# Feature blocks 2 to 4 of the first 512 tokens: two DMA transposes in place of twelve TensorE turns, and five weight columns written by GpSimd

## The chip, the cores and the metric

The kernel runs on one core of one Trainium2 chip. The metric is the time of one execution on the device, in microseconds (us), as a median over executions; lower is better. The profile's span, from the first to the last recorded work, is about 1.8 us shorter than this time (214.1 us in the run that took 215.9).

The profile lists five engines: TensorE (PE in the profile, 1413 matmuls before, with its weight loads as PEld), VectorE (DVE, 387 instructions), ScalarE (ACT, 185), GpSimd (POOL, 13) and SyncE (SP), which here only issues DMAs. Its timeline prints what an engine waited for, where the profile shows it. A line such as SPq is a DMA issue.

## The reference

2048 tokens of 640 features go through two branches, mixed token by token by a sigmoid gate.

```python
x = A_x                                             # [1, 2048, 640] bf16
g = sigmoid((x * gate_w).sum(-1, keepdims=True))
# branch A: state-space model with a diagonal complex state of 640
dt = exp(log_dt); Lam = Lambda_re + 1j * Lambda_im
Lam_bar = exp(dt * Lam)
Bu = einsum("bld,pd->blp", x, ((Lam_bar - 1) / Lam)[:, None] * (B_re + 1j * B_im))
h[t] = Lam_bar * h[t - 1] + Bu[:, t, :]
a = 2 * einsum("blp,dp->bld", h, C_re + 1j * C_im).real + x * Dskip
# branch B: a feed-forward layer of width 1728
b = gelu(x @ w1 + b1) @ w2 + b2
return g * a + (1 - g) * b
```

## The kernel before

The tokens are cut into four chunks of 512. The program's matmuls take the token features on the partitions, so every chunk needs its x transposed: `xT[c]` is 128 x 5 x 512, five feature blocks `kd` of 128. For chunks 1 to 3 a DMA transpose makes it. For chunk 0 nothing can start before it, so x is loaded plainly and TensorE transposes it by matmuls with an identity, called turns. Each turn leaves a 128 x 128 block in PSUM, and ScalarE or VectorE copies it to SBUF.

Feed-forward weights are loaded in three column groups, `w1a` (the first 768 columns), `w1b` and `w1c`, in the order of use. The gate weights become the last column of `w1c`, so that the gate's sum falls out of the last feed-forward matmul. Loads and parameter rows, in the order of issue:

```python
load_x0(nc.sync, 0, 1, 0, KA * P)              # tokens 0-127, features 0-255; KA = 2
load_w1a(nc.scalar, 0)
load_x0(nc.sync, 1, 2, 0, KA * P)
load_w1a(nc.scalar, 1)
load_x0(nc.sync, 2, 3, 0, KA * P)
load_x0(nc.scalar, 0, H, KA * P, D)            # features 256-639 of tokens 0-255
load_x0(nc.sync, 3, 4, 0, KA * P)
load_w1a(nc.sync, 2)
# ... clear prmA, prmB; warm up ScalarE's table
rows(nc.sync, prmA[0:KS, :], A_log_dt)
rows(nc.sync, prmA[KS:2 * KS, :], A_Lambda_im)
rows(nc.sync, prmA[2 * KS:3 * KS, :], A_Lambda_re)
load_x0(nc.sync, H, TPC, KA * P, D)            # features 256-639 of tokens 256-511
nc.sync.dma_start(out=w1a34[:], in_=...)       # w1a for blocks 3 and 4
rows(nc.sync, prmB[KS:NB, :], B_b1[0:(KF - 1) * P])
rows(nc.sync, prmB[0:KS, :], gate_w)
for kd in range(KD):
    nc.sync.dma_start(out=w1b[kd][:], in_=B_w1[kd * P:(kd + 1) * P, cut1:cut2])
# ... then w1c, B^T, ...
```

`prmA` holds log_dt and Lambda as rows; one small matmul with the identity (called the prmA matmul below) turns them into columns. In every trace PE passes this matmul before it goes on with the feed-forward layer, so when its rows are late, PE waits. The start of chunk 0 on PE, where `part(kd, a)` is feature block kd for 128 tokens and six column blocks of `w1a`:

```python
def turn(p, col, a, kd):
    nc.tensor.matmul(p[:, col:col + P], lhsT=xn[0][:, a, kd * P:(kd + 1) * P], rhs=ident[:], ...)
# ... blocks 0 and 1 of tokens 0-383
turn_rest(0, pA, (nc.scalar, KA, KD))          # three turns, one copy
nc.tensor.matmul(pP[:, 0:3 * KS], lhsT=prmA[:], rhs=ident[:, 0:3 * KS], ...)
part(0, 3)
turn_rest(1, bank(), (nc.vector, KA, KD))
part(1, 3)
part(2, 0); part(2, 1)
turn_rest(2, pA, (nc.scalar, KA, KD))
turn_rest(3, bank(), (nc.vector, KA, KD))
strip(KD - 1, 0, HT, False)                    # block 4, tokens 0-255
part(2, 2); part(2, 3)
# ... then block 4 of tokens 256-511 and block 3, Gelu, w1b, w1c, and at about 21 us x B^T
```

VectorE's instruction order is fixed when the kernel is built, by a small clock model: `ck.pe` adds an estimated time for each matmul, and an output combination (`ot`, one of two buffers) is put into VectorE's queue where the model says that its matmuls are done.

## Time and profile before

| | |
|---|---|
| time, median of 3 | 215.71 us (215.52 to 215.97) |
| profiled run, span | 215.9 us, 214.1 us |
| PE busy | 98% |
| first turn / prmA matmul / first w1b matmul | 3.28 / 7.40 / 12.80 us |
| first B^T matmul | 21.08 us |

Lines from the page of the kernel before: busy time of the engines, the granted TensorE clock in 40 slices, and the engines' shares of the chain that ended last.

```profile
PE 210.6 (98%) x1413; PEld 127.4 (59%) x1413; DVE 189.1 (88%) x387; ACT 102.7 (48%) x185; POOL 1.0 (0%) x13
PEclk9999999999999999999999999999999999999999
PE 98%; DVE 0%; issue 0%
```

The timeline of PE before, from 3.2 us on: start, duration, engine, line, operation, tiles and count; an idle time before the instruction would stand in brackets.

```profile
3.28 0.42 PE L233 MATMUL bank<-ident,xn 128*128 128x128 bf16 x2
...
4.46 1.16 PE L267 MATMUL bank<-xT,w1a 128*128 128x128 bf16 x9
5.42 0.42 PE L233 MATMUL bank<-ident,xn 128*128 128x128 bf16 x2
5.63 0.98 PE L267 MATMUL bank<-xT,w1a 128*128 128x128 bf16 x12
...
7.23 0.33 PE L233 MATMUL bank<-ident,xn 128*128 128x128 bf16 x3
7.40 0.17 PE L371 MATMUL bank<-ident,prmA 128*128 128x15 bf16 x1
...
12.80 4.48 PE L267 MATMUL bank<-xT,w1b 128*128 128x512 bf16 x20
...
21.08 0.81 PE L549 MATMUL bank<-xT,BT_re 128*128 128x512 bf16 x3
```

There is no bracket (the profile prints one from 0.15 us on): PE waits for nothing from the first turn on. The nine matmuls from 4.46 to 5.42 take (5.42 − 4.46) / 9 = 107 ns each; matmuls of the same shape take 57 ns from about 6 us on. The 512-column warm-up matmuls start 427 ns apart from 1.15 us on, those of the w1b stage 216. I read this as PE's clock doubling in between, at about 5.9 us, although the granted-clock row shows full speed throughout. The packed trace agrees: its first clock record, at full speed, starts at 5.92 us, and the row draws the time ahead of any record as full.

### The profile page before, as it was taken

The page shows a single profiled execution, that of the slowest core. Times are in us where ns is not written, and L with a number is a line of the kernel's source. Part 1 is how long each engine was busy: PE and PEld are TensorE (multiplying, and loading weights), DVE is VectorE, ACT ScalarE, POOL GpSimd, SP SyncE. Part 2 cuts the span into 40 slices and gives each one's busy share as a digit, 9 for nine tenths or more (in the row PEclk, how much of TensorE's full clock was granted, in tenths as well). Part 3 has the DMA queues.
Part 4 walks back from the last instruction along what each step waited for, and adds up shares of the span by engine and source line. Part 5 has one row for each costly group of instructions (what it writes and reads, how often), then busy time and mean ns, then how long its engine had stood idle before and what let it go on. Part 6 is the DMA issues. An engine that isn't in the chain of part 4 may idle for free.

```text
span 214.1 us, 3607 instructions
## 1 busy us (share of the span) xinstructions
PE 210.6 (98%) x1413; PEld 127.4 (59%) x1413; DVE 189.1 (88%) x387; ACT 102.7 (48%) x185; POOL 1.0 (0%) x13
## 2 busy tenths in 40 slices
PE   8999999999999999999999999999999999999994
PEld 5955444454475644775457777444457687676773
DVE  1589999999998999999999999999999999993153
ACT  3499856675759579203573210455683422305100
POOL 1000000000000000000000000000000000000000
PEclk9999999999999999999999999999999999999999
DMA  6869999999000000042000005100000000100011
GB/s 191 232 147 202 207 183 287 324 211 186 0 0 0 3 0 0 17 136 109 0 3 0 0 0 183 65 0 2 3 0 14 3 0 31 61 34 0 0 66 61
DMA packets 31571, 15.84 MB, mean 74 GB/s; under 512 B 22978, under 2 KB 31554, under 8 KB 31554
## 3 DMA queue, kind: packets, MB, share of 16 engines
q1 hardware_dynamic: 30850, 14.99, 29.2%
q10 hardware_dynamic: 704, 0.62, 0.9%
q8 instruction: 11, 0.18, 0.3%
q14 instruction: 6, 0.05, 0.1%
HBM read 7.48 MB, written 2.62 MB: 47 GB/s over the span
## 4 chain that ended last, share of the span: by engine, by line
PE 98%; DVE 0%; issue 0%
PE bank L267 27%; PE bank L608 27%; PE bank L667 20%; PE bank L549 20%; PE bank L230 1%; PE bank L624 1%; PE bank L293 1%; PE bank L233 1%; DVE ot L672 0%; PE bank L358 0%; PE bank L283 0%; PE bank L396 0%; PE bank L371 0%
## 5 line engine op out<-in xcount | busy, mean ns | idle before, releaser
L608 PE MATMUL bank<-w_sb,gel 128*128 128x384 bf16 (+1 forms) x416 | 57.9, 299 | 0.0
L608 PEld LDWEIGHTS <-gel 128*128 128x128 bf16 x416 | 40.3, 98 | 17.0 <-issue 0.8
L552 ACT ACTIVATE bu<-bank 128x512 bf16<-128x512 f32 x40 | 23.6, 597 | 37.3 <-PE bank L549 37.3
L272 ACT ACTIVATE gel<-bank,colB 128x512 bf16<-128x512 f32 x52 | 33.7, 693 | 10.4 <-PE bank L267 10.1
L667 PEld LDWEIGHTS <-hs 128*128 128x128 bf16 x330 | 31.7, 98 | 11.6
L503 DVE TENSOR_TENSOR_SCAN g<-r_c,carry,v 128x512 bf16<-128x512 f32 x30 | 37.2, 1268 | 0.0
L616 ACT ACTIVATE gb<-bank,gcol 128x384 f32<-128x384 f32 (+1 forms) x32 | 15.1, 526 | 32.9 <-PE bank L608 16.4
L267 PE MATMUL bank<-xT,w1a 128*128 128x512 bf16 (+2 forms) x180 | 28.6, 315 | 0.0
L667 PE MATMUL bank<-CT_re,hs 128*128 128x320 bf16 (+2 forms) x165 | 27.1, 295 | 0.0
L667 PE MATMUL bank<-CT_im,hs 128*128 128x320 bf16 (+2 forms) x165 | 27.1, 295 | 0.0
L672 DVE SCALAR_TENSOR_TENSOR ot<-bank,gcol,gb 128x320 bf16<-128x320 f32 (+2 forms) x33 | 17.4, 531 | 9.6 <-PE bank L667 8.2
L549 PE MATMUL bank<-xT,BT_re 128*128 128x512 bf16 x100 | 24.8, 379 | 0.0
L549 PE MATMUL bank<-xT,BT_im 128*128 128x512 bf16 x100 | 24.8, 379 | 0.0
L267 PEld LDWEIGHTS <-w1a 128*128 128x128 bf16 x180 | 15.5, 102 | 11.3
L267 PE MATMUL bank<-xT,w1b 128*128 128x512 bf16 x80 | 17.9, 379 | 0.0
L549 PEld LDWEIGHTS <-BT_im 128*128 128x128 bf16 x100 | 9.8, 98 | 11.8
L582 DVE TENSOR_TENSOR bank<-xn,Dbc 128x320 f32<-128x320 bf16 (+2 forms) x33 | 14.5, 480 | 2.1 <-ACT gb L616 2.1
L549 PEld LDWEIGHTS <-BT_re 128*128 128x128 bf16 x100 | 9.6, 98 | 11.0
L484 DVE TENSOR_TENSOR v<-wa,wb 128x512 bf16<-128x512 bf16 x40 | 15.2, 421 | 0.6
L597 ACT ACTIVATE bank<-b2bc 128x384 f32<-128x384 bf16 (+1 forms) x24 | 11.7, 529 | 7.6 <-DVE ot L672 7.6
L484 DVE TENSOR_TENSOR wa<-TCOS,g 128x1024 bf16<-128x1024 bf16 x20 | 13.7, 684 | 0.1
L267 PE MATMUL bank<-xT,w1c 128*128 128x512 bf16 x60 | 13.7, 379 | 0.0
(99 smaller groups left out, 166.1 us busy)
## 6 DMA issues: line engine op xcount, KB each, us to landing
out_dram<-ot SPq DMA_DIRECT2D x15, 160.0 KB, 1.8
w_sb<-in_B_w_dram SPq DMA_DIRECT2D x1, 2080.0 KB
xn<-in_A_x_dram SPq DMA_DIRECT2D x3, 640.0 KB
w1b<-in_B_w_dram SPq DMA_DIRECT2D x5, 128.0 KB, 3.6
w1c<-in_B_w_dram SPq DMA_DIRECT2D x5, 112.0 KB, 3.2
w1a<-in_B_w_dram ACTq DMA_DIRECT2D x2, 192.0 KB, 3.0
w1a<-in_B_w_dram SPq DMA_DIRECT2D x1, 384.0 KB, 3.7
xn<-in_A_x_dram SPq DMA_DIRECT2D x4, 64.0 KB, 3.6
```

The source lines that it names most:

```text
L267: nc.tensor.matmul(p[:, t0:t1], lhsT=w, rhs=xT[c][:, kd, t0:t1], start=(kd == 0) if first is None else first, stop=(kd == last), skip_grou ...
L272: nc.scalar.activation(out=gel[c][:, kf, :], in_=p[:, :], func=ACT.Gelu_apprx_tanh, bias=b1_c[:, kf:kf + 1])
L484: nc.vector.tensor_tensor(out=o, in0=a, in1=b, op=op)
L503: nc.vector.tensor_tensor_scan(s["g"][:, ri, :], r_c[:, ks:ks + 1].to_broadcast([P, CH]), s["v"][:, ri, :], init, ALU.mult, ALU.add)
L549: nc.tensor.matmul(p[:], lhsT=BT[ks >= KSA][:, kd, (ks % KSA if ks < KSA else ks - KSA) * P:][:, 0:P], rhs=xT[c][:, kd, :], start=(kd == 0 ...
L552: nc.scalar.activation(out=bu[:, ri, :], in_=p[:], func=ACT.Identity)
L582: dve_now(ck.pe, 0.45, lambda: nc.vector.tensor_tensor(out=p[:, 0:d1 - d0], in0=xn[c][:, a, d0:d1], in1=Dbc[:, d0:d1], op=ALU.mult))
L597: nc.scalar.activation(out=v, in_=src, func=ACT.Identity)
L608: nc.tensor.matmul(p[:, col:col + d1 - d0], lhsT=gel[c][:, kf, a * P:(a + 1) * P], rhs=w2_sb[:, kf, d0:d1], start=False, stop=False, skip_ ...
L616: nc.scalar.activation(out=gbs[ti][:, d0:d1], in_=p[:, col:col + d1 - d0], func=ACT.Identity, scale=gcol[:, 1, ti:ti + 1])
L667: nc.tensor.matmul(p[:, 0:d1 - d0], lhsT=hs[c][:, j, lo:lo + P], rhs=CT[:, j % KS, d0:d1], start=False, stop=(j == 2 * KS - 1), skip_group ...
L672: nc.vector.scalar_tensor_tensor(out=ot[:, d0:d1], in0=p[:, 0:d1 - d0], scalar=gcol[:, 0, ti:ti + 1], in1=gbs[ti][:, d0:d1], op0=ALU.mult, ...
```

## The change

Its intent is to take work from PE, which sets the time. Twelve turns go, their four PSUM copies with them, and blocks 2 to 4 come from two DMA transposes of 256 tokens each (196 KB). Since a block then arrives for 256 tokens or more at once, its matmuls can be wider. The first 192 KB of the plain x load are no longer ahead of the other loads; x for the later skip term is loaded much later. The three rows of `prmA` move to ACT's queue. GpSimd writes the gate columns, from the copy in SBUF, in place of five VectorE copies from PSUM.

```diff
-    load_x0(nc.scalar, 0, H, KA * P, D)
+    rows(nc.scalar, prmA[0:KS, :], A_log_dt)
     load_x0(nc.sync, 3, 4, 0, KA * P)
     load_w1a(nc.sync, 2)
     ... warm-up of ScalarE's table
-    rows(nc.sync, prmA[0:KS, :], A_log_dt)
-    rows(nc.sync, prmA[KS:2 * KS, :], A_Lambda_im)
-    rows(nc.sync, prmA[2 * KS:3 * KS, :], A_Lambda_re)
-    load_x0(nc.sync, H, TPC, KA * P, D)
-    nc.sync.dma_start(out=w1a34[:], in_=...)
+    for a in range(0, TPC, H):
+        nc.sync.dma_start_transpose(out=xT[0][:, KA:KD, a * P:(a + H) * P], in_=x2d[a * P:(a + H) * P, KA * P:D])
+    rows(nc.scalar, prmA[KS:2 * KS, :], A_Lambda_im)
+    rows(nc.scalar, prmA[2 * KS:3 * KS, :], A_Lambda_re)
+    load_w1a(nc.sync, 4)
+    load_w1a(nc.sync, 3)
     ... prmB rows and the five w1b loads as before
-    for kd in range(KD):                                    # w1c: five DMAs
+    for t, k0, k1 in ((w1c_lo, 0, 3), (w1c_hi, 3, KD)):     # w1c: two DMAs
     ... after w2:
+    load_x0(nc.sync, 0, TPC, KA * P, D)
     ... PE:
-    turn_rest(0, pA, (nc.scalar, KA, KD))
-    turn_rest(1, bank(), (nc.vector, KA, KD))
-    part(2, 0)
-    part(2, 1)
-    turn_rest(2, pA, (nc.scalar, KA, KD))
-    turn_rest(3, bank(), (nc.vector, KA, KD))
+    strip(2, 0, HT, False)
-    strip(KD - 1, 0, HT, False)
-    part(2, 2)
-    part(2, 3)
+    strip(2, HT, CH, False)
+    strip(4, 0, CH, False)
-            for j in range(KD):
-                nc.vector.tensor_copy(out=w1c[j][:, n1c - 1:n1c], in_=pA[:, j:j + 1])
     ... after the Gelus of w1a and of two w1b banks:
+    for t, k0, k1 in ((w1c_lo, 0, 3), (w1c_hi, 3, KD)):
+        nc.gpsimd.tensor_copy(out=t[:, :, n1c - 1:n1c], in_=colB[:, k0:k1].rearrange("p (k o) -> p k o", o=1))
```

One late load of x (chunk 3) is also split in two, and one early PSUM copy goes from ScalarE to VectorE.

More of the change, by code (lines that the diff above doesn't have):

```diff
@@ L83 @@
     xT = [const.tile([P, KD, CH], BF16, name=f"xT{c}") for c in range(NCH)]
-    w1a = [const.tile([P, cut1], BF16, name=f"w1a_{kd}") for kd in range(3)]
-    w1a34 = const.tile([P, 2, cut1], BF16, name="w1a34")
-    w1a += [w1a34[:, j, :] for j in range(2)]
+    w1a = [const.tile([P, cut1], BF16, name=f"w1a_{kd}") for kd in range(KD)]
     w1b = [const.tile([P, cut2 - cut1], BF16, name=f"w1b_{kd}") for kd in range(KD)]
-    w1c = [const.tile([P, n1c], BF16, name=f"w1c_{kd}") for kd in range(KD)]
+    w1c_lo = const.tile([P, 3, n1c], BF16, name="w1c_lo")
+    w1c_hi = const.tile([P, 2, n1c], BF16, name="w1c_hi")
+    w1c = [w1c_lo[:, j, :] for j in range(3)] + [w1c_hi[:, j, :] for j in range(2)]
     w2_sb = const.tile([P, KF - 1, D], BF16, name="w2_sb")
@@ L142 @@
     load_x0(nc.sync, 2, 3, 0, KA * P)
-    load_x0(nc.scalar, 0, H, KA * P, D)
+    nc.vector.memset(prmA[:], 0.0)
+    nc.vector.memset(prmB[:], 0.0)
+    rows(nc.scalar, prmA[0:KS, :], A_log_dt)
     load_x0(nc.sync, 3, 4, 0, KA * P)
     load_w1a(nc.sync, 2)
-    nc.vector.memset(prmA[:], 0.0)
-    nc.vector.memset(prmB[:], 0.0)
     warm = const.tile([P, 1], F32, name="warm")
     nc.scalar.activation(out=warm[:], in_=nc.const_aps.tensor(1.0, [P, 1], BF16), func=ACT.Exp)
-    rows(nc.sync, prmA[0:KS, :], A_log_dt)
-    rows(nc.sync, prmA[KS:2 * KS, :], A_Lambda_im)
-    rows(nc.sync, prmA[2 * KS:3 * KS, :], A_Lambda_re)
-    load_x0(nc.sync, H, TPC, KA * P, D)
-    nc.sync.dma_start(out=w1a34[:], in_=B_w1[3 * P:KD * P, 0:cut1].rearrange("(k p) f -> p k f", p=P))
+    for a in range(0, TPC, H):
[4 more added lines that the diff above has]
+    load_w1a(nc.sync, 3)
     rows(nc.sync, prmB[KS:NB, :], B_b1[0:(KF - 1) * P])
@@ L158 @@
         nc.sync.dma_start(out=w1b[kd][:], in_=B_w1[kd * P:(kd + 1) * P, cut1:cut2])
-    for kd in range(KD):
-        nc.sync.dma_start(out=w1c[kd][:, 0:F - cut2], in_=B_w1[kd * P:(kd + 1) * P, cut2:F])
+    for t, k0, k1 in ((w1c_lo, 0, 3), (w1c_hi, 3, KD)):
+        nc.sync.dma_start(out=t[:, :, 0:F - cut2], in_=B_w1[k0 * P:k1 * P, cut2:F].rearrange("(k p) f -> p k f", p=P))
     make_identity(nc, ident[:])
@@ L248, in turn_first @@
         turn(other, a * P, a, 1)
-        turned(nc.scalar, other, a * P, a, 1, 2)
+        turned(nc.scalar if a else nc.vector, other, a * P, a, 1, 2)
     turn_first(0, pA)
@@ L327, in strip @@
             ff1_mm(banks[kf], 0, kf, kd, t0, t1, first, 3)
-    def turn_rest(a, t, *parts):
-        for k in range(KA, KD):
-            turn(t, (k - KA) * P, a, k)
-        for engine, k0, k1 in parts:
-            turned(engine, t, (k0 - KA) * P, a, k0, k1)
     HB = CH // 2
@@ L397 @@
             nc.vector.tensor_copy(out=colB[:], in_=pA[:, 0:NB])
-            for j in range(KD):
-                nc.vector.tensor_copy(out=w1c[j][:, n1c - 1:n1c], in_=pA[:, j:j + 1])
-        for kd in (4, 3):
-            ff1_mm(banks[kf], 0, kf, kd, HT if kd == 4 else 0, CH, False, 3)
+        ff1_mm(banks[kf], 0, kf, 3, 0, CH, False, 3)
     for kf in range(FA):
@@ L700 @@
     fin_a(1)
-    load_xn(3)
+    load_xn(3, 0, H)
+    load_xn(3, H, TPC)
     ssm(3)
```

## The prediction

> **What bounds it now.** TensorE. The chain of waits puts 98% of the 214.1 us span on it; the list of waits shows none of it after the start; the granted clock is full. VectorE is busy 88%, yet always ahead: chunk 0's last state tile is written at 68 us and first read by the output matmuls at 86.8, the last CT fold ends 3.3 us before them. So only PE time counts, and the change alters PE's order only before 12.8 us (the first w1b matmul).
>
> **PE work removed.** From the PE timeline: twelve 128-column turns (six took 0.34 us, three 0.17) are 0.68 us. Feature block 2 goes from 24 matmuls of 128 columns (18 take 1.14 us, 63 ns each) to 12 of 256 (about 107 ns): 1.51 to 1.28 us. Block 4, 12 of 256 to 6 of 512, is even. [...] the trace has 57, 107, 216. Sum: 0.9 us, all on the chain. Also gone: four PSUM copies (ACT 0.49, DVE 0.56 us each), five DVE column copies (0.41 us) and two bank allocations. They let the sine chain and the first Gelu (13.6 us now) start 1 to 1.5 us earlier, which only keeps ACT and DVE ahead of PE.
>
> **What it adds: a new wait.** Blocks 2 and 4 of chunk 0 are then needed from the transposes at about 8.0 us (first half) and 8.7 (second), w1a4 at 9.35, w1a3 at 10.65. SP issues in order, and every DMA waits for the one eight before it (the order of instructions shows it; before, SP waited 0.4 us for w1a0 before its sixth issue). So transpose 1 issues at about 3.5 us, transpose 2 at 4.4, w1a4 at 5.4, w1a3 at 5.9. The first BT transpose (328 KB) took 5.2 us from issue to landing: 2.7 until its burst at about 290 GB/s, 1.2 in it, about 1.2 after. Estimate for 196 KB from these: 4.6 us, so landings at about 8.1 and 9.1, and w1a4, queued behind, at 9.6 to 10. [...] this trace has 290 GB/s in BT bursts against 370 to 390 in the plain w2 load, and gaps between transposes. I expect PE to wait about 0.5 us in all, mostly for transpose 2.
>
> Smaller risks: Lambda_re now leaves ACT's queue behind the warm-up and w1a1 (about 4.6 us against 4.17), needed at 7.2; w1b2 to w1b4 are issued after transpose 2 and w1a4 land, needed from 12.8 to 13.6. Smaller gain: 192 KB less in front of the first x tiles and w1a1, up to 0.3 us. Moved without effect: the rest of xn[0] (needed at 84 us), the GpSimd columns (needed at 20 us), the split late xn load.
>
> **Prediction.** 0.9 saved, 0.5 given back: 215.3 us, 8 in 10 between 214.6 and 216.2. Faster by over 2%: 0.01; within 2%: 0.97; slower by over 2%: 0.02.
>
> **What would show it.** First w1b matmul at about 12.4 us instead of 12.8, and every later PE stage earlier by the same amount, with unchanged lengths. PE waiting before the block-2 matmuls for the xT transposes (0.1 to 0.8 us in all). First Gelu near 12.2 us. If transposes land by 8.0 and 8.7, w1b starts at 11.9 and the time is near 214.8; if the second lands after 9.9, the change loses.
>
> **What would make it wrong.** Transposes much slower or faster beside plain loads than the BT ones; [...] a BT or w1b landing that turns into a second stall; PE, once earlier, catching up with DVE.

## More of the kernel before

SP's queue before, where the weights are issued:

```profile
5.25 0.40 SPq L154 DMA_DIRECT2D w1a<-in_B_w_dram  x1
...
6.71 2.26 SPq L158 DMA_DIRECT2D w1b<-in_B_w_dram  x5
```

## The result and the profile after

The kernel after took 215.89 us (median of 6 runs, 215.63 to 216.52). The kernel before took 215.86 us in the same rounds (6 runs, 215.52 to 216.16). The ratio is 1.0007 with a 95% interval of 0.9988 to 1.0025: the same time. Ratios in this document are the mean time of one kernel's runs over that of the other's runs of the same rounds, so not quite the ratio of the medians quoted.

The profiled execution after (216.52 us, the slowest of the six; span 214.7 us) has on its page:

```profile
PE 208.7 (97%) x1372; PEld 124.9 (58%) x1383; DVE 188.2 (88%) x381; ACT 102.3 (48%) x182; POOL 1.9 (1%) x15
DVE 70%; PE 22%; DMA 4%; issue 2%; ACT 1%; DVEq 0%
```

PE is less busy than before, but the chain that ended last no longer runs along PE alone: it leads through DVE and 4% of DMA. (11 of the 1383 matmuls have no record in this trace, so its busy time is a little low.) The PE timeline after:

```profile
4.25 0.67 PE L269 MATMUL bank<-xT,w1a 128*128 128x128 bf16 x9
...
5.78 0.83 PE L269 MATMUL bank<-xT,w1a 128*128 128x128 bf16 x12
7.18 0.17 PE L366 MATMUL bank<-ident,prmA 128*128 128x15 bf16 x1 [0.57 <-issue]
...
9.59 1.89 PE L269 MATMUL bank<-xT,w1a 128*128 128x512 bf16 x8 [0.24 <-DMA w1a<-in_B_w_dram]
...
11.99 1.46 PE L269 MATMUL bank<-xT,w1b 128*128 128x512 bf16 x6
13.96 3.20 PE L269 MATMUL bank<-xT,w1b 128*128 128x512 bf16 x14 [0.52 <-DMA w1b<-in_B_w_dram]
...
20.96 0.81 PE L538 MATMUL bank<-xT,BT_re 128*128 128x512 bf16 x2
```

The first w1b matmul starts 0.81 us earlier than before, but the first B^T matmul only 0.12 us earlier. Three waits stand in between or ahead: for the parameter rows, for a w1a load and for a w1b load. None is for a transpose. (The profile does not name what ended the first one, it prints "issue". That it was the rows is inferred: the matmul reads `prmA`, whose last row was issued at 4.31 us, 2.8 us before PE's weight load at 7.15, and in r9_gp below, whose rows landed by 6.3, there is no such wait.) Here the clock had doubled by 4.25 us: nine matmuls take (4.76 − 4.25) / 9 = 57 ns, where 4.76 us is the start of the next turn.

SP's queue after shows why w1b came late:

```profile
3.39 2.65 SPq L151 DMA_TRANSPOSE xT<-in_A_x_dram  x2
6.08 1.06 SPq L127 DMA_DIRECT2D w1a<-in_B_w_dram  x2
...
8.00 2.25 SPq L159 DMA_DIRECT2D w1b<-in_B_w_dram  x5
```

Two transposes hold the queue for 2.65 us, 1.3 us each, where a plain load of 192 KB holds it for 0.43. The w1b loads are issued from 8.00 us on and not from 6.71, 1.3 us later, while PE wants them earlier. The last of the five was issued at 8.54 us before and 9.82 after, and landed 4.4 us later in both traces, at 12.9 and 14.2. So in this pair the delay is one of issue and not of transfer (other traces: 3.6 and 4.0 us from issue to landing before, 4.1 to 4.6 after); experiments below test it.

Later in the program the kernel after lost a little more. VectorE after, around 98 and 135 us:

```profile
98.58 0.55 DVE L661 SCALAR_TENSOR_TENSOR ot<-bank,gcol,gb 128x320 bf16<-128x320 f32 x1 [1.42 <-DMA out_dram<-ot]
...
134.75 0.53 DVE L661 SCALAR_TENSOR_TENSOR ot<-bank,gcol,gb 128x320 bf16<-128x320 f32 x1
136.61 0.55 DVE L661 SCALAR_TENSOR_TENSOR ot<-bank,gcol,gb 128x320 bf16<-128x320 f32 x1 [1.32 <-DMA out_dram<-ot]
137.07 1.27 DVE L492 TENSOR_TENSOR_SCAN g<-r_c,carry,v 128x512 bf16<-128x512 f32 x1
...
174.55 0.90 DVE L571 TENSOR_TENSOR bank<-xn,Dbc 128x320 f32<-128x320 bf16 x2
```

The same stretch before:

```profile
134.20 0.52 DVE L672 SCALAR_TENSOR_TENSOR ot<-bank,gcol,gb 128x320 bf16<-128x320 f32 x1
134.64 1.27 DVE L503 TENSOR_TENSOR_SCAN g<-r_c,carry,v 128x512 bf16<-128x512 f32 x1
135.83 0.98 DVE L672 SCALAR_TENSOR_TENSOR ot<-bank,gcol,gb 128x320 bf16<-128x320 f32 x2
...
172.55 0.90 DVE L582 TENSOR_TENSOR bank<-xn,Dbc 128x320 f32<-128x320 bf16 x2
```

Before, a scan stands between the two output combinations; after, the combination comes first and must wait for its buffer's store. No line of the change touches this code. The build-time clock model saw other matmul widths at the start, its `ck.pe` moved by 0.036 us, and three places in VectorE's fixed order swapped. VectorE reached the seeding of the output banks at 174.55 us and not 172.55, and PE waited for it, its only wait for VectorE after the start:

```profile
175.10 0.84 PE L656 MATMUL bank<-CT_re,hs 128*128 128x320 bf16 x5 [0.52 <-DVE bank L571]
```

### The profile page after: what moved, and what is told of

Same layout as the page of the kernel before. It is cut to its first block, busy times and chain, and to the rows that moved or that the text cites. A ratio compares the mean times of both kernels' runs of the same rounds, so it can differ in the third digit from the quotient of the medians.

```text
span 214.7 us, 3526 instructions
## 1 busy us (share of the span) xinstructions
PE 208.7 (97%) x1372; PEld 124.9 (58%) x1383; DVE 188.2 (88%) x381; ACT 102.3 (48%) x182; POOL 1.9 (1%) x15
## 4 chain that ended last, share of the span: by engine, by line
DVE 70%; PE 22%; DMA 4%; issue 2%; ACT 1%; DVEq 0%
DVE g L492 19%; PE bank L656 10%; DVE wa L473 10%; DVE wb L473 10%; PE bank L597 7%; DVE v L473 6%; DVE hs L473 6%; DMA out_dram<-ot 4%; DVE bank L571 3%; PE bank L269 3%; DVE ot L661 3%; DVE CT_re L461 2%; DVE CT_im L461 2%; DVE g L421 1%; PE bank L232 1%
## 5 line engine op out<-in xcount | busy, mean ns | idle before, releaser
L656 PEld LDWEIGHTS <-hs 128*128 128x128 bf16 x330 | 31.7, 98 | 12.4 <-issue 0.7
L661 DVE SCALAR_TENSOR_TENSOR ot<-bank,gcol,gb 128x320 bf16<-128x320 f32 (+2 forms) x33 | 17.6, 535 | 12.4 <-PE bank L656 9.5
L269 PE MATMUL bank<-xT,w1a 128*128 128x512 bf16 (+2 forms) x158 | 27.0, 322 | 0.5 <-DMA w1a<-in_B_w_dram 0.2
L269 PEld LDWEIGHTS <-w1a 128*128 128x128 bf16 x162 | 13.8, 98 | 12.2 <-DMA w1a<-in_B_w_dram 0.3
L473 DVE TENSOR_TENSOR wb<-TSIN,g 128x1024 bf16<-128x1024 bf16 x20 | 13.7, 685 | 0.0
```

The source lines that it names most:

```text
L269: nc.tensor.matmul(p[:, t0:t1], lhsT=w, rhs=xT[c][:, kd, t0:t1], start=(kd == 0) if first is None else first, stop=(kd == last), skip_grou ...
L473: nc.vector.tensor_tensor(out=o, in0=a, in1=b, op=op)
L656: nc.tensor.matmul(p[:, 0:d1 - d0], lhsT=hs[c][:, j, lo:lo + P], rhs=CT[:, j % KS, d0:d1], start=False, stop=(j == 2 * KS - 1), skip_group ...
L661: nc.vector.scalar_tensor_tensor(out=ot[:, d0:d1], in0=p[:, 0:d1 - d0], scalar=gcol[:, 0, ti:ti + 1], in1=gbs[ti][:, d0:d1], op0=ALU.mult, ...
```

## The experiments

Twelve runs were made, in four calls; runs of one call are on one chip and share their runs of the kernel before, whose medians were 215.46, 215.93, 215.60 and 215.39 us. Differences of a few tenths of a microsecond in a median are not more than scatter here, so I rest the argument on stages of the traces. In each profiled run the span splits in two at the first B^T matmul: the start up to it, and the rest, which is the same work in all kernels. Where a quoted expectation gives a theory the letter E, it is the moving clock step, told below.

| run | kernel | clock doubles at about | first B^T matmul | rest of span |
|---|---|---|---|---|
| first look | before | 5.9 us | 21.08 | 193.0 |
| r5_before | before | 6.7 | 21.55 | 193.1 |
| r11_before_look | before | 3.9 to 4.2 | 20.44 | 193.1 |
| first look | after | 3.6 | 20.96 | 193.7 |
| r1_again | after | 4.2 | 20.65 | 193.3 |
| r2_dveorder | after, old VectorE order | 4.0 | 21.01 | 193.1 |
| r3_ot3 | after, three ot buffers | 6.4 | 20.73 | 193.1 |
| r4_w1btwo | after, w1b in two DMAs | 6.5 | 20.61 | 194.5 |
| r6_cols | before, columns by GpSimd | 6.2 | 21.20 | 193.2 |
| r9_gp | after, parameters by GpSimd | 5.1 | 19.87 | 194.1 |
| r10_gp_w1b | r9 and w1b in two DMAs | 6.7 | 20.64 | 193.1 |
| r12_gp_sp | r9 and w2 in four DMAs | 6.0 | 20.34 | 193.2 |

"Rest" is the span less the column to its left (214.7 − 20.96 = 193.7). The clock's step is the start of the trace's first full-clock record, and agrees within 0.1 us with the spacing of 128-column matmuls, 107 ns before it and 57 after; r11_before_look has no such record, so there it is read from the spacing alone. (Some expectations below were written with a rougher reading, 4.2 us for all three early steps.)

### The unaltered kernels once more

r1_again is the kernel after, r5_before and r11_before_look are the kernel before, without an edit.

> The changed kernel, unaltered. Theory A: its runs fall in two groups. Where VectorE loses time to late output DMAs (2.7 us in the profiled run), the first output matmuls of chunk 2 wait about 0.5 us and the run takes about 216.4; where it does not, the run takes 215.6 to 215.9. In every profile the first w1b matmul starts near 12.0 us, then PE waits about 0.5 us for w1b and reaches the BT matmuls at 20.9 to 21.0, only 0.1 us before the kernel before. Rival B: one group, scatter of the chip alone; ratio 1.000 and the profile shows the same 0.5 us wait at chunk 2 every time.

> The kernel before, unaltered, for a second profile. Theory E: the runs of one kernel differ mostly by the moment at which PE's matmuls of 128 columns go from 107 ns to 57 ns apart (5.9 us in the first profile of before; 4.2 us in three and 6.5 us in two profiles of the changed kernel). Where it comes near 4.2 us here, BT matmuls start at 20.3 to 20.5 and the run takes 215.0 to 215.3; where it comes at 5.9 us or later, they start at 21.1 or later and the run takes 215.9 or more. So before's fast runs form two groups 0.8 us apart. Rival: the groups come from DMA landings and the BT start does not go with the moment of the step.

> The kernel before once more, for one profile. Theory E: with the clock step near 4.2 us BT starts at 20.2 to 20.5 and the run takes 215.0 to 215.4; with a step at 5.9 us or later 21.0 to 21.6 and 215.9 to 216.4.

Measured: r1_again 215.99 us (215.65 to 216.62), ratio 1.0024 (0.9999 to 1.0049). r5_before 216.06 us (215.48 to 216.43), ratio 1.0003 (0.9982 to 1.0023), so no bias of the comparison shows. r11_before_look 215.23 us. The two groups expected of r1_again do not stand out in its six runs, and its first B^T matmul came at 20.65 us and not at 20.9 to 21.0; the expectations for r5_before and r11_before_look held.

The kernel before is not one time but a range, and its traces say why. Lines of r5_before (216.35 us in its profiled run):

```profile
4.63 1.17 PE L267 MATMUL bank<-xT,w1a 128*128 128x128 bf16 x9
...
21.55 0.81 PE L549 MATMUL bank<-xT,BT_re 128*128 128x512 bf16 x3
```

and of r11_before_look (215.23 us), the same stages:

```profile
4.45 0.67 PE L267 MATMUL bank<-xT,w1a 128*128 128x128 bf16 x9
...
20.44 0.81 PE L549 MATMUL bank<-xT,BT_re 128*128 128x512 bf16 x3
```

Nine matmuls take 1.17 us in one and 0.67 in the other; the clock doubled early in r11 and late in r5, and the first B^T matmul differs by 21.55 − 20.44 = 1.11 us. The times differ by 216.35 − 215.23 = 1.12, and the rest of the span is equal. The other two traces with this PE work fit in between: 5.9 us and 21.08, and r6_cols with 6.2 and 21.20. So the kernel before follows the clock's step all the way. The step moves from run to run without any edit: 3.9 to 4.2, 5.9 and 6.7 us in the three traces of the kernel before, and 3.6 to 6.7 us over all kernels. What sets its moment is not shown.

The kernel after does not follow the step in the same way. Its four early-stepping and late-stepping traces (first look, r1 and r2 at 3.6 to 4.2; r3 at 6.4, equal to the kernel after up to 90 us) have the first B^T matmul at 20.96, 20.65, 21.01 and 20.73. After a late step that is 0.8 us earlier than r5_before, whose first turn itself started 0.18 us later (3.47 us against 3.29), and 0.5 earlier than r6_cols, with the PE work of before, a start at 3.29 and a step at 6.2. After an early step it is 0.2 to 0.6 us later than r11_before_look, the only early trace of before, although the first turn there started 0.2 us later. With an early step, PE runs into the landing of loads and waits for them; with a late one PE itself is slow and waits little (r3: only 0.20 us, for w1b). Early waits were 0.57, 0.84 and 0.76 us for the parameter rows, 0.24, 0.19 and 0.24 for w1a. The landings set the pace of the start.

### How much PE work is gone: both kernels with the data already there

The chain's start is held on PE until all early loads have landed. The same edit goes into both kernels: VectorE runs 16 timed operations, PE runs 46 dummy matmuls meanwhile, and then one matmul that needs VectorE's result. In both traces the clock is up at the start of the chain: nine 128-column matmuls take 0.50 us from 17.12 us on, 56 ns each.

```diff
+    tim = const.tile([P, D], F32, name="tim")
+    go = const.tile([P, P], BF16, name="go")
+    nc.vector.memset(tim[:], 0.0)
+    for _ in range(16):
+        nc.vector.tensor_tensor(out=tim[:], in0=tim[:], in1=tim[:], op=ALU.mult)
+    nc.vector.tensor_copy(out=go[:], in_=tim[:, 0:P])
+    for _ in range(46):
+        nc.tensor.matmul(pA[:, 0:512], lhsT=ones(P), rhs=ones(512), start=True, stop=True)
+    nc.tensor.matmul(pA[:, 0:P], lhsT=go[:], rhs=ones(P), start=True, stop=True)
```

> The kernel before, held: a chain of sixteen VectorE operations (about 14 us) ahead of the first turn, with 46 more dummy matmuls, so that all loads have landed and PE's clock is up before the first turn. Theory E and F (in the first 14 us the changed kernel runs at the pace of DMA landings and of the clock step, not of PE's work): from the first turn to the first BT matmul 16.9 to 17.2 us without any PE wait, and the scatter of the fast runs falls below 0.5 us. To be compared with r8_hold_after.

> The changed kernel, held in the same way. Theory F (the PE work saved, 0.9 us, is real and is hidden by landings): from the first turn to the first BT matmul 0.8 to 1.0 us less than in r7_hold_before, and the whole run 0.7 to 1.0 us faster than r7_hold_before. Rival G (the longer matmuls and the transposes save PE nothing): both equal within 0.2 us.

The PE timeline of r7_hold_before, first turn and first B^T matmul:

```profile
16.24 0.28 PE L242 MATMUL bank<-ident,xn 128*128 128x128 bf16 x2
...
33.04 1.24 PE L558 MATMUL bank<-xT,BT_re 128*128 128x512 bf16 x5
```

and of r8_hold_after:

```profile
16.25 0.27 PE L244 MATMUL bank<-ident,xn 128*128 128x128 bf16 x2
...
32.09 1.24 PE L547 MATMUL bank<-xT,BT_re 128*128 128x512 bf16 x5
```

With no wait for a load in it, this stretch is 16.80 us before and 15.84 us after. The change removes 0.96 us of PE work. The whole times show it too: five of six runs of r7 lie at 227.81 to 227.85 us, three of r8 at 226.90 to 226.93, 0.90 us less. The other runs, one of r7 (229.32) and three of r8 (228.53 to 228.54), are 1.5 and 1.6 us longer. I have no profile of such a run, but the record lists the mean granted clock of each: 0.991 to 0.993 in these four, 0.998 to 1.000 in the other eight. A clock lower by 0.7 to 0.9% over 227 us is 1.6 to 2.0 us, the size of the gap; what lowered it stays open. So the medians of this pair prove nothing; I use the stretch and the low groups. (The expected scatter below 0.5 us failed by these runs, and the stretch before is just under the expected 16.9 to 17.2.)

### The gate columns alone

r6_cols is the kernel before with w1c in two DMAs and the columns written by GpSimd.

```diff
-            for j in range(KD):
-                nc.vector.tensor_copy(out=w1c[j][:, n1c - 1:n1c], in_=pA[:, j:j + 1])
+    for t, k0, k1 in ((w1c_lo, 0, 3), (w1c_hi, 3, KD)):
+        nc.gpsimd.tensor_copy(out=t[:, :, n1c - 1:n1c], in_=colB[:, k0:k1].rearrange("p (k o) -> p k o", o=1))
```

> The kernel before with only the other part of the change: w1c in two DMAs and the gate weight columns written by GpSimd. All theories: no PE wait for GpSimd, the five VectorE copies (0.4 us) gone, PE stages of the same length, time equal to before's within 0.2 us. If this run is slower by 0.3 us or more, the columns have a part in the missing gain.

It took 215.79 us (215.17 to 216.23), ratio 0.9995 (0.9976 to 1.0014), no PE wait. This part neither gives nor costs anything that can be seen.

### Late losses: VectorE's order and the output buffers

r2_dveorder is the kernel after with the constant that the clock model had lost:

```diff
+    ck.pe += 0.036
     for kf in range(FA):
         ff1_act(banks[kf], 0, kf)
```

r3_ot3 is the kernel after with a third output buffer, so that a combination need not wait for a store:

```diff
-            ot = fwork.tile([P, D], BF16, name="ot", bufs=2)
+            ot = fwork.tile([P, D], BF16, name="ot", bufs=3)
```

> Changed kernel, with 0.036 us added to the build-time clock so that VectorE's instruction order is that of the kernel before (three swaps undone). Theory A1 (the swap that puts the third output tile before a scan makes VectorE wait for the output DMA): VectorE's wait near 135 us vanishes, its lag at 172 us is below 1.5 us, PE does not wait before chunk 2's output matmuls, and no run is above 216.1; median 215.6. Rival A2 (late output DMAs are chance, order has no part): same spread as r1_again.

> Changed kernel with three output tiles in place of two, so that VectorE does not wait for an output DMA. Theory A: no VectorE wait on out_dram in the middle of the kernel, no PE wait at chunk 2, median 215.6 and highest below 216.1. If the slow runs stay, the DMA wait is not what makes them. It is not expected to gain more than 0.3 us over the median of the changed kernel, since PE reaches BT only 0.1 us earlier.

r2_dveorder took 215.37 us (215.06 to 216.17), ratio 0.9994 (0.9966 to 1.0022); r3_ot3 215.70 us (215.33 to 216.26), ratio 1.0010 (0.9985 to 1.0035). Neither trace has a VectorE wait for a store, neither has a PE wait at the output of chunk 2, and both have 193.1 us for the rest of the span, as before. The kernel after has 193.7 and 193.3, with a PE wait at that point of 0.52 us in the first trace; in r1_again that stage started 0.16 us late. So the late loss is real in the traces (that stage starts 0.16 to 0.68 us late, counted from the first B^T matmul), and goes with either cure. In the medians it is at the edge: r2 is the lowest of the first call, but its interval holds 1. Both expectations also set 216.1 us as a ceiling, and the highest runs were 216.17 and 216.26, so the slowest runs are not shown to come from the late loss.

### The w1b wait

r4_w1btwo is the kernel after with w1b loaded by two DMAs of three and two blocks, to shorten SP's issue:

```diff
-    for kd in range(KD):
-        nc.sync.dma_start(out=w1b[kd][:], in_=B_w1[kd * P:(kd + 1) * P, cut1:cut2])
+    for t, k0, k1 in ((w1b_lo, 0, 3), (w1b_hi, 3, KD)):
+        nc.sync.dma_start(out=t[:], in_=B_w1[k0 * P:k1 * P, cut1:cut2].rearrange("(k p) f -> p k f", p=P))
```

> Changed kernel with w1b in two DMAs (three blocks, two blocks) in place of five: same bytes, SP issues done about 1.3 us earlier. Theory C (SP's issue time, 2.65 us of it for the two transposes, delays w1b): the wait of 0.5 us for w1b vanishes or halves, BT matmuls start at 20.3 to 20.6, time 0.3 to 0.6 us below r1_again. Rival D (the DMA engines are behind with the bytes, transposes moving slower than plain loads): w1b blocks 3 and 4 land at 13.9 to 14.2 as before and the BT start stays at 20.9 or later.

SP's queue and PE's timeline in r4_w1btwo:

```profile
7.95 0.41 SPq L161 DMA_DIRECT2D w1b_lo<-in_B_w_dram  x1
8.41 0.49 SPq L161 DMA_DIRECT2D w1b_hi<-in_B_w_dram  x1
```

```profile
12.32 1.47 PE L271 MATMUL bank<-xT,w1b_lo 128*128 128x512 bf16 x6
13.63 1.03 PE L271 MATMUL bank<-xT,w1b_hi 128*128 128x512 bf16 x4
```

The issue of w1b takes 0.95 us in place of 2.25, the bytes are the same, and no w1b wait appears after the first w1b matmul. About 0.2 us is lost just ahead of it: the first w1b matmul starts 0.85 us after the last w1a group and not 0.65, and its weight load waits for the larger first DMA, which landed 4.3 us after issue. This supports SP's issue time as the cause of the w1b wait. It is not a clean proof: the clock's step was late in this run (6.5 us), so PE also came later. r9_gp below is the better test. The time to issue is not small beside the DMA here: in the kernel after, two transposes held the issuing queue for 2.65 us, with landings of 3.2 and 4.0 us after issue (2.6 to 3.2 us for the plain 192 KB w1a loads of the same trace).

The whole kernel was slower all the same, 216.91 us (216.84 to 217.02), ratio 1.0063 (1.0040 to 1.0086). The start was not the cause (20.61 us). The rest of the span was 194.5 us, 1.4 more than the usual 193.1. It has a PE wait of 0.37 us at the output of chunk 2, as in the kernel after, and a long end: 4.07 us from the start of the last group of matmuls to the end of the span, against 3.1 to 3.4 in the traces of other runs.

### Parameters on a queue of their own, and the long end

r9_gp is the kernel after with the five parameter rows issued by GpSimd and the constant of r2; r10_gp_w1b adds the two w1b loads of r4; r12_gp_sp is r9_gp with the w2 load cut in four.

```diff
-    rows(nc.scalar, prmA[0:KS, :], A_log_dt)      # and the four other rows on scalar and sync
+    rows(nc.gpsimd, prmA[0:KS, :], A_log_dt)      # all five, after the memsets of tf
+    rows(nc.gpsimd, prmA[KS:2 * KS, :], A_Lambda_im)
+    rows(nc.gpsimd, prmA[2 * KS:3 * KS, :], A_Lambda_re)
+    rows(nc.gpsimd, prmB[KS:NB, :], B_b1[0:(KF - 1) * P])
+    rows(nc.gpsimd, prmB[0:KS, :], gate_w)
+    ck.pe += 0.036
 # r12_gp_sp also:
-    for k0, k1 in ((0, KF - 1),):
+    for k0, k1 in ((0, 4), (4, 7), (7, 10), (10, KF - 1)):
```

> Changed kernel with the five small parameter rows on GpSimd's queue (off the SP and ACT queues, so the transposes no longer wait for a DMA eight places earlier), and VectorE's order as in r2_dveorder. Theory F: the wait for prmA (0.57 to 0.84 us where the clock steps up early) is gone, prmA is read before 7.0 us there, SP issues w1b from about 7.0 us instead of 8.0, the w1b wait goes, BT matmuls start at 20.1 to 20.6, the run takes 215.0 to 215.5 with all runs under 216.0: 0.2 to 0.8 us faster than before. Rival (something else holds the first 14 us): BT start stays at 20.7 to 21.0.

> r9_gp with w1b in two DMAs as well. Theory C: BT matmuls at or before r9_gp's, within 0.2 us. Open is the 0.8 us that r4_w1btwo showed after its last output DMA; if the two-DMA form of w1b makes it, this run shows it again (about 0.8 us above r9_gp with PE ending at the same time); if not, it came from elsewhere.

> The kernel of r9_gp (the changed kernel, with the five parameter rows loaded by the GpSimd queue and the build-time constant that keeps VectorE's old order) with the second big weight of the feed-forward loaded in four DMAs, so that SyncE's queue has 58 issues and not 55. Theory (an instruction fetch of the last stores' queue falls after the last output in kernels with 55 or fewer rows there, and the end waits for it): first B^T matmul between 19.9 and 20.7 us without a PE wait, the end 3.1 to 3.4 us after the last matmul (4.31 in r9_gp), span 213.0 to 213.7, median 0.2 to 0.8 us below the kernel before (ratio 0.996 to 0.999). Rival (the long end of r9_gp has another cause): the end stays at 4.0 us or more, the ratio at 1.002 to 1.006, and the cause is open.

The start of r9_gp is the best of all traces. Its w1b issue on SP's queue, and its PE timeline:

```profile
6.87 2.33 SPq L154 DMA_DIRECT2D w1b<-in_B_w_dram  x5
```

```profile
6.97 0.17 PE L366 MATMUL bank<-ident,prmA 128*128 128x15 bf16 x1
7.00 4.08 PE L269 MATMUL bank<-xT,w1a 128*128 128x128 bf16 x33
...
11.59 4.48 PE L269 MATMUL bank<-xT,w1b 128*128 128x512 bf16 x20
...
19.87 1.24 PE L539 MATMUL bank<-xT,BT_re 128*128 128x512 bf16 x5
```

PE waits for nothing, and the first B^T matmul is at 19.87 us, 1.2 us before the first trace of before (whose clock stepped 0.8 us later). The transposes still hold SP's queue (2.66 us), but without the parameter rows w1b is issued from 6.87 us, 1.13 earlier than in the kernel after; its last block lands at 11.9 and not at 14.2 (about 1.05 us of that is the earlier issue, the rest a faster transfer), and PE, which comes for it earlier than in any other trace, does not wait. Yet r9_gp took 216.05 us (215.77 to 218.29), ratio 1.0052 (1.0017 to 1.0088), where 215.0 to 215.5 was expected. Again the end is long: 4.31 us from the last matmul group. In the DMA view of r9_gp, by queue, packets, megabytes and share of 16 engines, for 211.4 to 211.7 us and then for 212.0 to 212.2 us (nothing moved between):

```profile
q10 hardware_dynamic: 135, 0.03, 46.8%
q14 instruction: 1, 0.01, 9.2%
...
q10 hardware_dynamic: 9, 0.00, 4.8%
```

The last output store, on q10, has 144 packets. In the midst of them falls one fetch of instructions, q14, and the last nine packets, one sixteenth of the store, come 0.3 us after the others. r4_w1btwo looks alike: a fetch among the store's packets, and nine late packets from 213.3 us on. Every other trace that I looked at has the 144 packets in one piece. In those of the kernels before and after, this fetch falls between 203 and 209 us, well ahead of the end. The profile counts 60 issues on SP's queue before, 58 after, 55 in r4 and 56 in r9 (the quoted expectation has one fewer for each kernel); so I took it that with fewer issues the last fetch comes later. r12_gp_sp tests this by three more DMAs for the same bytes, which has nothing to do with the start or the end otherwise. In r12_gp_sp, for 207.5 to 208.0 us and then for 211.9 to 212.2:

```profile
q8 instruction: 1, 0.02, 10.9%
q14 instruction: 1, 0.01, 3.8%
...
q10 hardware_dynamic: 144, 0.03, 49.9%
```

The fetch is back at 207.5 us, the store is in one piece, and the end is 213.5 − 210.17 = 3.33 us (210.17 is the start of the last matmul group). The run took 215.29 us (214.87 to 215.48), ratio 0.9986 (0.9967 to 1.0004): its first B^T matmul at 20.34 us lay 0.47 later than in r9_gp (its first x tile landed late, the first turn started at 3.67 and not 3.29, and the clock stepped 0.9 us later), and the time was still 0.76 us lower, or 0.55 when the runs of before in the two calls, 0.21 apart, are allowed for. The gain of 0.2 to 0.8 us over the kernel before that was expected did not come: it is 0.1 in the medians.

r10_gp_w1b, with 53 issues, has the fetch late too, but at 212.4 us, as the last of the store's packets end; its end is 3.24 us and its time 215.54 us (214.98 to 215.70), ratio 0.9996 (0.9978 to 1.0014). In this trace a late fetch alone costs nothing, then; falling among the last store's packets goes with the long end. (Its first B^T matmul, 20.64 us, missed the expected 0.2 us from r9's; the clock's step came at 6.7 and not 5.1.) The late packets account for about 0.4 of the one microsecond in r9. The rest lies behind the last packet: from there to the end it is 1.84 us in r9 and 1.63 in r4, and 1.2 to 1.4 in every other trace. What fills it stays open, and so does r9's spread up to 218.29 us.

No version beats the kernel before by more than the intervals leave open. r12_gp_sp comes nearest, and its interval still holds 1.

## Why the prediction was right, and where it was not

**The total and the class: right.** 215.3 us with 214.6 to 216.2 was said; 215.89 was measured, against 215.71 at first and 215.86 in the same rounds. But the range was wide enough to hold no change at all as well, and the gain of 0.4 us that the prediction forecast did not come (ratio 1.0007). That the total is right owes more to this width than to the mechanism; the points below tell what failed.

**PE is the bound, and 0.9 us of PE work goes: right.** The held pair measured 0.96 us. The spacings that it read from the trace, 57 and 216 ns for 128 and 512 columns, are also those of the traces after.

**"I expect PE to wait about 0.5 us in all, mostly for transpose 2": the place was wrong, and the size too small.** No trace of the kernel after has a PE wait for a transpose. The prediction had the landings at 8.1 and 9.1 us; they came 4.0 us after the issue at 3.39 and 3.2 us after the one at 4.77, so at 7.4 and 8.0. The step that failed is the 4.6 us for 196 KB, an estimate scaled from a B^T transpose of 328 KB that took 5.2. What did wait: the parameter rows (0.57 to 0.84 us with an early clock step), w1a4 (0.19 to 0.24, as the estimate of its landing had it) and w1b (0.20 to 0.52 in three traces; in r1_again no wait is marked, but the w1b stage takes 4.70 us and not 4.48). The sum in the first trace is 0.57 + 0.24 + 0.52 = 1.33 us. The first and the third had been listed as smaller risks, with the right mechanism: Lambda_re behind the warm-up on ACT's queue, w1b behind the transposes on SP's. I had put no number on either.

**"Every later PE stage earlier by the same amount, with unchanged lengths": wrong.** The w1b stage starts 0.81 us earlier, at 11.99 us and so earlier than the 12.4 predicted, then loses 0.52 to its own loads. The prediction tied "w1b starts at 11.9" to 214.8 us; that link failed.

**What the prediction didn't see: the clock's step.** It costed the turns at full clock and took the start of one trace as fixed. The start of the kernel before moves by 1.11 us between runs, with the step, as much as the whole saving. With a late step the kernel after keeps 0.5 to 0.8 us of it at the first B^T matmul; with an early step it is 0.2 to 0.6 us behind the one early trace of before, since the loads set the pace. How often each happens in untraced runs I can't tell.

**"Only keeps ACT and DVE ahead of PE": wrong.** The first Gelu did come early (12.13 us; 12.2 predicted, 13.6 before), but VectorE's lead was lost at about 98 and 136 us, to waits for stores. One came from a swap in its fixed order. The last sentence, "PE, once earlier, catching up with DVE", named the symptom, not this cause. It cost 0.2 to 0.7 us of span, and with the old order or a third buffer it was gone.

**The GpSimd columns without effect: right** (r6_cols, 0.9995). The granted clock did not fall: it is 1.0 in all six runs.

So the balance is: 0.96 us of work off PE; with an early clock step all of it and some tenths more, with a late one a smaller part, given back at the start to loads that came no earlier; and a few tenths lost later by VectorE's delay.

## What to carry to other kernels

Work taken off the bounding engine at the start of this program was worth only as much as the loads behind it could follow (0.96 us of PE work went, and the time stayed the same, ratio 1.0007): list for every load the time of issue, not only of landing, since two DMA transposes held the issuing queue here for 2.65 us and moved all later weights back by 1.3 (by 0.2 once the parameter rows had left that queue, in r9_gp). Before judging a change of half a percent, profile the old kernel more than once and see how far the stage in question moves by itself; a pair of kernels held until all data is there measures the work alone. And where an instruction order is computed at build time, compare the orders of the whole program after a change to its first microseconds.
